# Scores of units 8 to 15 in pairs on six PSUM banks, and superblock 0's three output tiles one after another

## The chip, the cores and the metric

The kernel runs on one core of one Trainium2 chip. A core has TensorE (PE, matmuls), ScalarE (ACT), VectorE (DVE), GpSimd (POOL), and SyncE (SP), whose queue here issues nearly all DMAs. Matmuls write PSUM, which has eight banks; a bank holds 512 fp32 values in each of 128 partitions. The metric is the device time of one execution in microseconds (us). Times are medians over runs; the profile is of one execution.

## The reference

Attention with four sink keys and a window of 128, then a feed-forward layer on its output:

```python
scores = (q @ k.T) / sqrt(64)                 # 4 batches x 8 heads, 768 x 768
keep   = (key < 4) | ((0 <= row - key) & (row - key < 128))
a      = softmax(where(keep, scores, -1e9))   # over keys
x      = (a @ v), heads side by side          # 3072 x 512
h      = x @ w_in                             # 3072 x 2048
g      = h * sigmoid(beta * h)
out    = g @ w_out                            # 3072 x 512
```

## The kernel before

**Units and superblocks.** Attention is cut into 32 units: unit n is one batch, one pair of heads and one half (384 rows) of the sequence. Four units (the four head pairs) fill one superblock T = n // 4 of 384 rows of x. For each superblock there are 16 hidden groups (`hidden`: four 128x384 matmuls, L765, into one bank; `tanh` on ScalarE, L773; `gate` on VectorE, L788, which writes one slice of g) and three tiles of x @ w_out (`project`: 16 matmuls of 128x512, L815, added up in one bank, then an eviction, L823 on ScalarE or L827 on VectorE, and a store, L830). The sigmoid is taken as a tanh with beta halved, and the half is made good in the eviction.

**One unit.** Loads (L449, L457, L440), casts to bf16 on GpSimd (`cast`, L508, L511), a transpose of q and k to qkT: on TensorE for units below 12 (`transpose_in`, L531, copied out of PSUM by L540), by a DMA from unit 12 on (L515). Then the scores (64 rows, two heads side by side on the two halves of TensorE's rows), an exponential on ScalarE, a mask multiplied in on VectorE, for the second half of a sequence also the sink scores (L560, L563), `attend` (L703, L714, into the bank `av`), `normalise` (L723, L725), and a transpose of the output into xT: on TensorE (`transpose_out`, L742, copied by L746) below unit 12, by a DMA (L734) from 12 on.

**How scores are issued.** There are three forms. Units 0 to 11 use `scores` in two parts, "a" and "b": six matmuls (L587), and one exponential (L594) and one mask (L605) of 128x768 for each part. Units 12 to 15 use `scores_at_once`: eight matmuls in the four banks of `s_ps` (L624), one exponential (L631) and one mask (L680) of 128x1536. From unit 16 on `scores_pair` takes two units at a time on six banks, three for each (L660), with two exponentials (L672) and two masks (L680).

**PSUM.** Six banks are named s0, s1, tr, av, h0, h1; the other two are acc0 and acc1. Hidden groups of superblocks 0 and 1 go through acc0, acc1, h0 and h1, those of later ones through h0, h1, s0 and s1. Tiles are added up in acc0 and acc1; those of superblock 0 in acc0, acc1 and h1.

**Order.** The program is written in slots s. In one slot stand at most one hidden group, three projections, and the steps of units that fall on it (`EARLY`, `FIRST` and `STEPS`: "in", "sink", "a", "b", "av", "out"), with the casts and loads set for that slot. A planner (`Prog.order`) then lists all engines' instructions by estimated start times; what it lists is fixed when the kernel is built, and each engine runs its list in order, with semaphore waits where data or a buffer comes from another engine. In slots 0 to 31 the hidden groups of superblocks 0 and 1 run; in slots 32 to 47 superblock 0's tiles, three matmuls a slot; from 48 on hidden groups of one superblock run beside the tiles of the one before it.

Of the kernel before, what the change touches and what calls it, by code (L numbers as in the profile page):

```python
# [6 lines left out]
AF = mybir.ActivationFunctionType  # L7
# [39 lines left out]
BANK_B = {4: 's', 5: 'h', 6: 'h', 7: 'h'}  # L47
BANK_S = {4: 't', 5: 'h', 6: 'h', 7: 't'}

TURN_IN = {4: 'act', 5: 'dve', 6: 'dve', 7: 'dve', 8: 'dve', 9: 'act', 10: 'dve', 11: 'dve'}  # L50
TURN_OUT = {4: 'dve', 5: 'dve', 6: 'act', 7: 'act', 8: 'dve', 9: 'dve', 10: 'dve', 11: 'dve'}

LAST = 384

# [13 lines left out]
LATE, PAIRED = 2, 16  # L68
STEPS = {0: "in", 1: "sink", 2: "a", 3: "b", 5: "av", 7: "out"}


class Node:
# [225 lines left out]
def bass_streamingllm_window__then__act_swish_beta_kernel(  # L298
# [74 lines left out]
    def act(n):  # L373
        return {"busy": 80.0 + 0.81 * n, "lag": 140.0}
# [56 lines left out]
    def place(n):  # L431

        return n // 8, n % 4, n // 4 % 2, n % 4
# [173 lines left out]
            m[:, first:first + w].unsqueeze(1).to_broadcast([128, 2, w]), ALU.mult),  # L607
           r=[("E", n % 2, c), *names], w=[("E", n % 2, c)], **dve(780.0))

    def scores_at_once(n):  # L610

        _, _, half, pb = place(n)
        pieces = []
        for x, (kb, qb) in enumerate(BLOCKS[half]):
            if x % 4 and pieces[-1][1] == kb:
                pieces[-1] = (*pieces[-1][:3], pieces[-1][3] + 1)
            else:
                pieces.append((x, kb, qb, 1))
        with P.together("pe"):
            for x, kb, qb, nq in pieces:  # L620
                for hh in range(2):
                    rows = slice(64 * hh, 64 * hh + 64)
                    bank, at = 2 * hh + x // 4, x % 4
                    op("pe", lambda e, kb=kb, bank=bank, qb=qb, at=at, nq=nq, rows=rows: e.matmul(  # L624
                        s_ps[:, bank, 128 * at:128 * (at + nq)],
                        qkT[pb][rows, kb // 3, 1, kb % 3 * 128:kb % 3 * 128 + 128],
                        qkT[pb][rows, half, 0, qb % 3 * 128:(qb % 3 + nq) * 128], start=True, stop=True),
                       r=[("qT", pb, half), ("qkT", pb, kb // 3)], w=[("s0", "s1", "tr", "av")[bank]],
                       busy=27.0 * nq + 20.0, lag=260.0)
        z = n % 2  # L630
        op("act", lambda e: e.activation(  # L631
            E[z][:, :, :, :].rearrange("p c h x -> p c (h x)"),
            s_ps[:, :, :].rearrange("p (h b) x -> p h (b x)", h=2)[:, :, 0:768], AF.Exp,
            bias=0.0, scale=SCALE),
           x=["s0", "s1", "tr", "av"], w=[("E", z, 0), ("E", z, 1)], **act(1536))

    def scores_pair(n):

        banks = {n: ("av", "h0", "h1"), n + 1: ("s0", "s1", "tr")}
# [45 lines left out]
    def attend(n):  # L685
        _, hp, half, pb = place(n)
        z = n % 2
        where = {}
        for c, tiles in enumerate(CHUNKS[half]):
            at = 0  # L690
            for kb, qb, nq in tiles:
                for x in range(nq):
                    where[kb, qb + x] = [(c, hh, at) for hh in range(2)]
                    at += 128
        if n >= XBAR:

            where = {t: [(hh, x // 3, x % 3 * 128) for hh in range(2)]
                     for x, t in enumerate(BLOCKS[half])}
        with P.together("pe"):
            for mm in range(3):  # L700
                m, at = 3 * half + mm, mm * 2 * D1
                if half == 1:
                    op("pe", lambda e, at=at, mm=mm: e.matmul(  # L703
                        av_ps[:, at:at + 2 * D1], E_sink[z][:, mm * 128:mm * 128 + 128],
                        v_sink[:, n // 8 * 4 + hp, :, :].rearrange("p h e -> p (h e)"),
                        start=True, stop=False, skip_group_check=True),
                       r=[("E_sink", z), "v_sink", ("v_sink", 0), ("v_sink", 1)], w=["av"],
                       **pe(130))
                for hh in range(2):
                    kbs = range(m + 1) if half == 0 else (m - 1, m)  # L710
                    for x, kb in enumerate(kbs):
                        c, h2, col = where[kb, m][hh]
                        node = op("pe", lambda e, at=at, hh=hh, kb=kb, c=c, h2=h2, col=col, first=(half == 0 and x == 0),
                           last=(x == len(kbs) - 1): e.matmul(  # L714
                            av_ps[:, at + hh * D1:at + hh * D1 + D1], E[z][:, c, h2, col:col + 128],
                            v_aug[pb][:, kb, hh, :], start=first, stop=last, skip_group_check=True),
                           r=[("E", z, c), ("v_aug", pb, kb // 3)], w=["av"], **pe(65))
        return node
# [212 lines left out]
    casts = {FIRST[n - 2] + (3 if n % 2 and n - 2 >= PAIRED else 1): n for n in range(10, NU)}  # L931
    casts.update({EARLY[n - 2]["sink"]: n for n in range(6, 8)})
    slots = {*range(S_END + NM), *(at for steps in EARLY.values() for at in steps.values())}
    for s in sorted(slots):
        i = s if 0 <= s < S_P0 and s == int(s) else s - NM if S_PIPE <= s < S_END else None
# [6 lines left out]
        here += [(n, STEPS[s - FIRST[n]]) for n in range(8, NU)  # L942
                if s - FIRST[n] in STEPS and not (n >= PAIRED and n % 2 and STEPS[s - FIRST[n]] == "av")]
        here += [(n, "av") for n in range(PAIRED + 1, NU, 2) if s - FIRST[n] == 5 + LATE]
        later = []
        if i is not None and i >= S_P0 and any(n >= XBAR and step in ("sink", "b") for n, step in here):
            gate(i)
            i = None
        for n, step in here:
            half = place(n)[2]  # L950
            if step == "in" and n < XBAR:
                transpose_in(n, eng=TURN_IN.get(n, "dve"))
            if step == "sink" and half == 1:
                scores_sink(n, *((h_ps[:, 0, :], "h0") if BANK_S.get(n) == "h" else (tr_ps, "tr") if BANK_S.get(n) == "t" else (s_ps[:, 0, :], "s0") if n < PAIRED
                                 else (tr_ps, "tr")))
            if step == "b" and XBAR <= n < PAIRED:
# [6 lines left out]
            if step in ("a", "b") and n < XBAR:  # L963
# [12 lines left out]
        if s in casts:  # L976
            n = casts[s]
            cast(n)
            if n in (12, 13):
                load(n + 2)  # L980
        if s == EARLY[5]["a"]:
            for x in range(4, 8):
                cast_w(x)
# [25 lines left out]
        if s == EARLY[7]["sink"]:  # L1009
# [69 lines left out]
```

## Time and profile before

| | us |
|---|---|
| time, median of 3 runs | 225.46 (224.97 to 225.82) |
| time of the profiled execution | 225.03 |
| its span, first to last instruction | 223.2 |
| TensorE busy | 218.2 |
| ScalarE busy | 143.7 |
| VectorE busy | 128.4 |
| GpSimd busy | 74.3 |

The granted TensorE clock was 1.0 throughout. Rows of groups read: line, engine, operation, output <- inputs, shape, count; busy time and mean time of one; idle time before them and what ended it. Rows of the timeline read: start, length, engine, line, operation, output <- inputs, shape, count, and in brackets the idle time of the engine before it. The tile `six` stands for the six banks. Matmuls are pipelined, so their lengths overlap, and the distance between starts is what counts. Rows of the stages read: busy time of each engine in ten us with the number of instructions, granted clock, DMA share and GB/s. In the rows of DMA issues the last number is the median time from issue to landing.

### The profile page before, as it was taken

How to read it: one execution, taken by the hardware profiler on the slowest of the kernel's cores; microseconds unless marked ns; L12 is line 12 of the kernel's file. 1: busy time of each engine (PE TensorE's matmuls, PEld its weight loads, DVE VectorE, ACT ScalarE, POOL GpSimd, SP SyncE). 2: the span in 40 equal slices, each digit the busy share in tenths (PEclk: the TensorE clock that was granted, in tenths of full speed). 3: DMA queues.
4: the chain of work that ended last, by engine and by line, in shares of the span. 5: the costliest groups of instructions: out<-in, count | busy, mean ns of one | idle time of the engine just before them, and what ended most of it. 6: DMA issues, size and time to landing. Idle time of an engine off the chain costs nothing.

```text
span 223.2 us, 4521 instructions
## 1 busy us (share of the span) xinstructions
PE 218.2 (98%) x1757; PEld 122.1 (55%) x1757; DVE 128.4 (58%) x257; ACT 143.7 (64%) x227; POOL 74.3 (33%) x149
## 2 busy tenths in 40 slices
PE   7999999999999999999999999999999999999995
PEld 4554557555554556555565556564656555555443
DVE  5365778998734267476194448584938466254300
ACT  2777997896255477666596568596767594465411
POOL 7675767997432314453201513700000000000000
DMA  6999999997779999996996899742020202111022
GB/s 190 299 332 318 324 351 268 339 387 166 166 177 202 238 259 189 256 237 145 241 251 165 199 274 206 152 131 82 18 68 7 78 15 68 50 47 47 14 83 94
DMA packets 95437, 39.79 MB, mean 178 GB/s; under 512 B 81960, under 2 KB 88376, under 8 KB 95416
## 3 DMA queue, kind: packets, MB, share of 16 engines
q1 hardware_dynamic: 93760, 38.68, 68.6%
q10 hardware_dynamic: 1656, 0.83, 1.3%
q8 instruction: 14, 0.23, 0.4%
q14 instruction: 7, 0.06, 0.1%
HBM read 27.30 MB, written 6.29 MB: 151 GB/s over the span
## 4 chain that ended last, share of the span: by engine, by line
PE 88%; SPq 4%; DMA 3%; ACT 2%; issue 0%; DVE 0%; DVEq 0%
PE acc L815 35%; PE six L765 30%; PE acc L765 5%; PE six L714 5%; DMA wst<-in_moe_w_in_dram 3%; PE six L660 3%; SPq L457 2%; SPq L449 2%; PE six L587 2%; PE six L815 2%; PE six L703 1%; PE acc L796 1%; PE six L560 1%; PE six L531 1%; ACT th L773 1%; PE six L624 1%
## 5 line engine op out<-in xcount | busy, mean ns | idle before, releaser
L815 PE MATMUL acc<-w_out,g 128*128 128x512 bf16 x352 | 88.5, 379 | 0.0
L773 ACT ACTIVATE th<-six,beta_half 128x384 f32<-128x384 f32 x106 | 60.6, 583 | 29.8 <-PE six L765 23.9
L765 PE MATMUL six<-xT,w_in 128*128 128x384 bf16 x424 | 79.5, 326 | 0.0
L788 DVE SCALAR_TENSOR_TENSOR g<-th,six 128x384 bf16<-128x384 f32 x106 | 56.6, 550 | 26.0 <-ACT th L773 24.2
L765 PEld LDWEIGHTS six<-xT,w_in 128*128 128x128 bf16 x424 | 40.6, 98 | 29.9 <-issue 0.6
L815 PEld LDWEIGHTS acc<-w_out,g 128*128 128x128 bf16 x352 | 32.7, 98 | 33.7 <-issue 1.8
L680 DVE TENSOR_TENSOR E<-E,mask_all 128x1536 bf16<-128x1536 bf16 x20 | 19.9, 997 | 36.1 <-ACT E L672 26.8
L672 ACT ACTIVATE E<-six 128x1536 bf16<-128x1536 f32 x16 | 22.3, 1448 | 12.1 <-PE six L660 12.0
L508 POOL CAST qk<-q_stage 128x384 bf16<-128x384 f32 x32 | 16.5, 516 | 28.5 <-DMA q_stage<-in_q_dram 16.0
L511 POOL CAST v_aug<-v_stage 128x384 bf16<-128x384 f32 x32 | 17.3, 551 | 20.3 <-DMA v_stage<-in_v_dram 12.5
L594 ACT ACTIVATE E<-six 128x768 bf16<-128x768 f32 x24 | 19.1, 817 | 5.8 <-PE six L587 5.8
L508 POOL CAST qk<-k_stage 128x384 bf16<-128x384 f32 x31 | 17.3, 561 | 13.1 <-DMA k_stage<-in_k_dram 12.6
L823 ACT ACTIVATE out_sb<-acc 128x512 f32<-128x512 f32 x22 | 13.0, 595 | 10.7 <-PE acc L815 10.5
L714 PE MATMUL six<-v_aug,E 128*128 128x65 bf16 x384 | 19.3, 193 | 0.3
L714 PEld LDWEIGHTS six<-v_aug,E 128*128 128x128 bf16 x384 | 17.2, 97 | 4.0 <-ACT E L594 0.7
L765 PE MATMUL acc<-xT,w_in 128*128 128x384 bf16 x88 | 18.5, 327 | 0.3 <-DVE g L788 0.3
L725 DVE TENSOR_TENSOR o_norm<-six,rden 128x384 bf16<-128x384 f32 x32 | 17.8, 557 | 1.2
L788 DVE SCALAR_TENSOR_TENSOR g<-th,acc 128x384 bf16<-128x384 f32 x22 | 11.7, 548 | 4.6 <-ACT th L773 4.5
L773 ACT ACTIVATE th<-acc,beta_half 128x384 f32<-128x384 f32 x22 | 12.7, 591 | 2.3 <-PE acc L765 2.1
L563 ACT ACTIVATE E_sink<-six 128x384 bf16<-128x384 f32 x16 | 7.9, 497 | 5.7 <-PE six L560 5.7
L765 PEld LDWEIGHTS acc<-xT,w_in 128*128 128x128 bf16 x88 | 7.4, 97 | 4.9 <-DVE g L788 0.8
L723 DVE RECIPROCAL rden<-six 128x6 f32<-128x6 f32 x32 | 6.1, 192 | 6.6 <-PE six L714 6.5
(74 smaller groups left out, 160.0 us busy)
## 6 DMA issues: line engine op xcount, KB each, us to landing
out_dram<-out_sb SPq DMA_DIRECT2D x23, 256.0 KB, 2.6
wst<-in_moe_w_in_dram SPq DMA_DIRECT2D x8, 512.0 KB, 6.6
wst<-in_moe_w_out_dram SPq DMA_DIRECT2D x8, 512.0 KB, 8.6
q_stage<-in_q_dram SPq DMA_DIRECT2D x8, 384.0 KB, 4.0
k_stage<-in_k_dram SPq DMA_DIRECT2D x8, 384.0 KB, 4.2
v_stage<-in_v_dram SPq DMA_DIRECT2D x8, 384.0 KB, 4.4
v_stage<-in_v_dram SPq DMA_DIRECT2D x30, 96.0 KB, 4.5
q_stage<-in_q_dram SPq DMA_DIRECT2D x12, 192.0 KB, 5.0
```

Source lines behind the costliest of these rows:

```text
L508: op(eng, lambda e, x=x, name=name: e.tensor_copy(qk16[z][:, x, :, :, :], view(name)), r=[(name + "_stage", pb, half, hh) for hh in range( ...
L511: op("gp", lambda e: e.tensor_copy(v_aug[pb][:, 3 * half:3 * half + 3, :, 0:D], view("v")), r=[("v_stage", pb, half, hh) for hh in range(2 ...
L594: op("act", lambda e: e.activation(E[n % 2][:, c, :, 0:at], bank[:, 0:2, 0:at], AF.Exp, bias=0.0, scale=SCALE), x=[f"{name}0", f"{name}1"] ...
L672: op("act", lambda e, u=u, first=first: e.activation(E[u % 2][:, :, :, :].rearrange("p c h x -> p (c h x)"), six[:, first:first + 3, :].re ...
L680: op("dve", lambda e: e.tensor_tensor(both, both, mask_all[:, half, :].unsqueeze(1).to_broadcast([128, 2, 768]), ALU.mult), r=[("E", z, 0) ...
L714: last=(x == len(kbs) - 1): e.matmul(av_ps[:, at + hh * D1:at + hh * D1 + D1], E[z][:, c, h2, col:col + 128], v_aug[pb][:, kb, hh, :], sta ...
L725: op("dve", lambda e: e.tensor_tensor(o_norm[o][:, :, :, :].rearrange("p m h d -> p (m h) d"), src[:, :, 0:D], rden[z][:, :].unsqueeze(2). ...
L765: return op("pe", lambda e: e.matmul(bank, w_in16[:, c, m * 128:(m + 1) * 128], xT[:, c, T * TT:(T + 1) * TT], start=(c == 0), stop=(c == 3)),
L773: op("act", lambda e: e.activation(th[i % 3][:, :], bank, AF.Tanh, bias=0.0, scale=beta_half[:, m:m + 1]), x=[name], r=["beta"], w=[("th", ...
L788: op("dve", lambda e: e.scalar_tensor_tensor(g[T % 2][:, m, :], th[i % 3][:, :], 1.0, bank, ALU.add, ALU.mult), r=[("th", i % 3)], x=[name ...
L815: node = op("pe", lambda e: e.matmul(bank, g[T % 2][:, m, t * 128:(t + 1) * 128], w_out16[:, m, :], start=(m == 0), stop=(m == NM - 1)), r ...
L823: op("act", lambda e: e.activation(out_sb[z][:, :], bank, AF.Copy, bias=0.0, scale=0.5), x=[name], w=[("out_sb", z)], **act(NOUT))
```

## The change

- Units 8 to 15 take their scores by `scores_pair`, in pairs (8, 9), (10, 11), (12, 13) and (14, 15). `PAIRED` is 8; `scores_at_once` is gone; `attend` reads E in the pair's layout from unit 8 on.
- Superblock 0's tiles no longer run side by side on acc0, acc1 and h1, but one after another on acc1, acc0 and acc1, as those of the other superblocks do; the third is evicted by VectorE.
- The transposed q and k of units 8 to 11 are copied by ScalarE (they were VectorE's, but for unit 9's), in slots of their own (`TURNED`). The output copies of units 8 and 11 move to ScalarE.
- The slots of units from 8 on, of their casts (`CASTS`) and of some loads are set anew. The hidden groups of slots without attention steps, the weights, the transposes and the last superblock are as they were. The planner's list changes with all this.

```diff
-TURN_IN = {... 8: 'dve', 9: 'act', 10: 'dve', 11: 'dve'}
-TURN_OUT = {... 8: 'dve', 9: 'dve', 10: 'dve', 11: 'dve'}
+TURN_IN = {... 8: 'act', 9: 'act', 10: 'act', 11: 'act'}
+TURN_OUT = {... 8: 'act', 9: 'dve', 10: 'dve', 11: 'act'}
...
-FIRST = {8: 17, 9: 23, 10: 27, 11: 28}
-FIRST.update({12: 39, 13: 43, 14: 46, 15: 50, 16: 60, 17: 60})
-FIRST.update({n: (68, 76, 83, 92, 99, 108, 116)[n // 2 - 9] for n in range(18, NU)})
+TURNED = {8: 16, 9: 22, 10: 23, 11: 31}
+
+FIRST = {n: (31, 37, 42, 49, 60, 68, 76, 83, 90, 99, 106, 112)[n // 2 - 4] for n in range(8, NU)}
+CASTS = {6: EARLY[4]['sink'], 7: EARLY[5]['sink'], 10: 17, 11: 23, 12: 24, 13: 32, 14: 39, 15: 44, 16: 50, 17: 54}
+CASTS.update({n: FIRST[n - 2] + (3 if n % 2 else 1) for n in range(18, NU)})
...
-LATE, PAIRED = 2, 16
-STEPS = {0: "in", 1: "sink", 2: "a", 3: "b", 5: "av", 7: "out"}
+LATE, PAIRED = 2, 8
+STEPS = {0: "in", 1: "sink", 3: "b", 5: "av", 7: "out"}
...
-    def scores_at_once(n):
...
-        if n >= XBAR:
+        if n >= PAIRED:
             where = {t: [(hh, x // 3, x % 3 * 128) for hh in range(2)]
...
-    at = {16: 38, 17: 44, 18: 50, 19: 55, 24: 70, 25: 76, 26: 84, 27: 89}
+    at = {16: 43, 17: 44, 18: 49, 19: 55, 24: 73, 25: 78, 26: 84, 27: 85}
...
-        if i is not None and i >= S_P0 and any(n >= XBAR and step in ("sink", "b") for n, step in here):
+        if i is not None and i >= S_P0 and any(n >= PAIRED and step in ("sink", "b") for n, step in here):
             gate(i)
...
-            if step == "b" and XBAR <= n < PAIRED:
-                scores_at_once(n)
-                later.append(lambda n=n: mask_at_once(n))
             if step == "b" and n >= PAIRED and n % 2 == 0:
                 scores_pair(n)
...
-        if s == 34:
+        if s == 33:
...
-        if S_P0 <= s < S_PIPE:
-
-            for t, (bank, name, eng) in enumerate(
-                    ((acc[0][:, :], "acc0", "act"), (acc[1][:, :], "acc1", "act"),
-                     (h_ps[:, 1, :], "h1", "dve"))):
-                done = project(0, t, s - S_P0, bank, name, eng)
-        elif s >= S_PIPE:
-            T = (s - S_PIPE) // NM + 1
+        if s >= S_P0:
+            T = (s - S_P0) // NM
             for x in range(3 * (s % NM), 3 * (s % NM) + 3):
                 a = (3 * T + x // NM + 1) % 2
...
-                done = project(T, x // NM, x % NM, acc[a][:, :], f"acc{a}")
+                done = project(T, x // NM, x % NM, acc[a][:, :], f"acc{a}",
+                               "dve" if T == 0 and x // NM == 2 else "act")
```

More of the change, by code (lines that the diff above doesn't have):

```diff
@@ L48 @@
 BANK_S = {4: 't', 5: 'h', 6: 'h', 7: 't'}
-TURN_IN = {4: 'act', 5: 'dve', 6: 'dve', 7: 'dve', 8: 'dve', 9: 'act', 10: 'dve', 11: 'dve'}
-TURN_OUT = {4: 'dve', 5: 'dve', 6: 'act', 7: 'act', 8: 'dve', 9: 'dve', 10: 'dve', 11: 'dve'}
+TURN_IN = {4: 'act', 5: 'dve', 6: 'dve', 7: 'dve', 8: 'act', 9: 'act', 10: 'act', 11: 'act'}
+TURN_OUT = {4: 'dve', 5: 'dve', 6: 'act', 7: 'act', 8: 'act', 9: 'dve', 10: 'dve', 11: 'act'}
 LAST = 384
@@ L608, in mask @@
            r=[("E", n % 2, c), *names], w=[("E", n % 2, c)], **dve(780.0))
-    def scores_at_once(n):
[L612 to L635, printed above, removed]
     def scores_pair(n):
@@ L926, in bass_streamingllm_window__then__act_swish_beta_kernel @@
         sink_keys(n, ended)
-    at = {16: 38, 17: 44, 18: 50, 19: 55, 24: 70, 25: 76, 26: 84, 27: 89}
+    at = {16: 43, 17: 44, 18: 49, 19: 55, 24: 73, 25: 78, 26: 84, 27: 85}
     loads = {t + 2 * x: (n, name) for n, t in at.items() for x, name in enumerate("qkv")}
-    casts = {FIRST[n - 2] + (3 if n % 2 and n - 2 >= PAIRED else 1): n for n in range(10, NU)}
-    casts.update({EARLY[n - 2]["sink"]: n for n in range(6, 8)})
     slots = {*range(S_END + NM), *(at for steps in EARLY.values() for at in steps.values())}
@@ L941, in bass_streamingllm_window__then__act_swish_beta_kernel @@
         here = [(n, step) for n in EARLY for step in EARLY[n] if EARLY[n][step] == s]
-        here += [(n, STEPS[s - FIRST[n]]) for n in range(8, NU)
-                if s - FIRST[n] in STEPS and not (n >= PAIRED and n % 2 and STEPS[s - FIRST[n]] == "av")]
-        here += [(n, "av") for n in range(PAIRED + 1, NU, 2) if s - FIRST[n] == 5 + LATE]
+        here += [(n, "in") for n in TURNED if TURNED[n] == s]
+        for n in range(8, NU):
+            step = STEPS.get(s - FIRST[n] - (LATE if n % 2 and s - FIRST[n] >= 5 else 0))
+            if step in ("sink", "b", "av") or step == "out" and n < XBAR:
+                here.append((n, step))
         later = []
-        if i is not None and i >= S_P0 and any(n >= XBAR and step in ("sink", "b") for n, step in here):
+        if i is not None and i >= S_P0 and any(n >= PAIRED and step in ("sink", "b") for n, step in here):
             gate(i)
@@ L962, in bass_streamingllm_window__then__act_swish_beta_kernel @@
                 later.append(lambda n=n: mask_at_once(n + 1))
-            if step in ("a", "b") and n < XBAR:
+            if step in ("a", "b") and n < PAIRED:
                 scores(n, "ab".index(step), *((h_ps, "h") if BANK_B.get(n) == "h" and step == "b" else (s_ps, "s")))
@@ L975, in bass_streamingllm_window__then__act_swish_beta_kernel @@
                     transpose_out(n, eng=TURN_OUT.get(n, "dve"))
[L976 to L980, printed above, removed]
+        for n in CASTS:
+            if CASTS[n] == s:
+                cast(n)
+                if n in (12, 13):
+                    load(n + 2)
         if s == EARLY[5]["a"]:
```

## The prediction

> **What bounds the kernel now.** I read the page first: busy times, the 40 slices, the chain that ended last and the two largest groups.
>
> ```profile
> span 223.2 us, 4521 instructions
> PE 218.2 (98%) x1757; PEld 122.1 (55%) x1757; DVE 128.4 (58%) x257; ACT 143.7 (64%) x227; POOL 74.3 (33%) x149
> PE   7999999999999999999999999999999999999995
> PE 88%; SPq 4%; DMA 3%; ACT 2%; issue 0%; DVE 0%; DVEq 0%
> L815 PE MATMUL acc<-w_out,g 128*128 128x512 bf16 x352 | 88.5, 379 | 0.0
> L765 PE MATMUL six<-xT,w_in 128*128 128x384 bf16 x424 | 79.5, 326 | 0.0
> ```
>
> TensorE (PE) has work in every slice after the first, is 88% of the chain, and its two big matmul groups show no idle time before them. A busy share says little about pipelined matmuls, so next came the timeline of TensorE alone, by start times: from one row's start to the next is what the first one cost.
>
> ```profile
> 39.53 0.81 PE L765 MATMUL six<-xT,w_in 128*128 128x384 bf16 x4
> 40.27 0.34 PE L587 MATMUL six<-qkT 64*128 64x384 bf16 x2
> 40.54 0.34 PE L531 MATMUL six<-ident,qk 128*128 128x128 bf16 x3
> 40.72 1.46 PE L765 MATMUL acc<-xT,w_in 128*128 128x384 bf16 x8
> ...
> 56.35 0.81 PE L815 MATMUL six<-w_out,g 128*128 128x512 bf16 x3
> 57.09 0.34 PE L587 MATMUL six<-qkT 64*128 64x256 bf16 x4
> 57.36 0.54 PE L714 MATMUL six<-v_aug,E 128*128 128x65 bf16 x12
> ...
> 62.48 0.38 PE L815 MATMUL six<-w_out,g 128*128 128x512 bf16 x1
> 62.79 0.50 PE L624 MATMUL six<-qkT 64*128 64x128 bf16 x8
> 63.23 0.60 PE L815 MATMUL acc<-w_out,g 128*128 128x512 bf16 x2
> ...
> 90.83 1.67 PE L815 MATMUL acc<-w_out,g 128*128 128x512 bf16 x7
> 92.44 0.83 PE L660 MATMUL six<-qkT 64*128 64x256 bf16 x14
> 93.21 2.98 PE L815 MATMUL acc<-w_out,g 128*128 128x512 bf16 x13
> 96.02 0.53 PE L714 MATMUL six<-v_aug,E 128*128 128x65 bf16 x12
> 96.39 1.24 PE L815 MATMUL acc<-w_out,g 128*128 128x512 bf16 x5
> 97.47 2.76 PE L765 MATMUL six<-xT,w_in 128*128 128x384 bf16 x16
> 100.06 0.53 PE L714 MATMUL six<-v_aug,E 128*128 128x65 bf16 x12
> ...
> 116.62 1.67 PE L815 MATMUL acc<-w_out,g 128*128 128x512 bf16 x7
> 118.23 0.84 PE L660 MATMUL six<-qkT 64*128 64x256 bf16 x18
> 119.00 2.98 PE L815 MATMUL acc<-w_out,g 128*128 128x512 bf16 x13
> ```
>
> No row brackets an idle time: here TensorE waits for nobody. A 128x512 matmul costs 2.81/13 = 0.216 us (93.21 to 96.02), a 128x384 one 2.59/16 = 0.162 (97.47 to 100.06), three transposes 0.18 (40.54 to 40.72), a whole `attend` 0.37 (96.02 to 96.39). So this stage is worth what its TensorE instructions cost, and a change gains only by issuing cheaper ones, and only while nobody makes TensorE wait.
>
> **What the change does to TensorE.** Up to the row at 39.53 both kernels issue the same instructions, on every compute engine and on SP's queue. After it, the counts of hidden matmuls, projections, transposes and `attend` are unchanged; what changes is how scores are issued. A score matmul has 64 rows, and each stretch of them costs more than its columns, where TensorE enters and where it leaves it:
>
> - `scores`, first part: the four matmuls at 39.53 cost 4 x 0.162, to 40.18; the transposes start at 40.54: 0.36. Second part: 57.36 - (56.35 + 3 x 0.216) = 0.36. Units 8 to 11 have two each: 8 x 0.36 = 2.88 us.
> - `scores_at_once`: 63.23 - (62.48 + 0.216) = 0.534. Units 12 to 15: 4 x 0.534 = 2.14 us.
> - `scores_pair`, both forms: 93.21 - (90.83 + 7 x 0.216) = 0.865 with 14 matmuls, 119.00 - (116.62 + 7 x 0.216) = 0.865 with 18. It replaces two units at a time, four times: 3.46 us.
>
> Sum: 2.88 + 2.14 - 3.46 = **1.56 us less**. It is all fixed cost: a first part's 384 columns, two row groups side by side, would need 0.162 us, so some 0.2 us per stretch is entering and leaving, and 12 stretches become 4 (8 x 0.2 = 1.6).
>
> The Trainium skill says why there is such a cost: in "TensorEngine Tiling (Array Packing)", section Tiling Modes, changing the tiling mode drains TensorE. "TensorE: Matmul & The Clock Gate", section Single matmul latency, puts the fixed part of a lone warm matmul at about 166 ns; as an estimate from these pages, 16 switches fewer would be worth 2.7 us and give 222.8 before any stall. The rows, 0.2 for a switch in and out together, decide for 1.56.
>
> **What must stay covered.** After a pair, ScalarE and VectorE of the kernel before go:
>
> ```profile
> 93.26 2.79 ACT L672 ACTIVATE E<-six 128x1536 bf16<-128x1536 f32 x2 [1.64 <-PE six L660]
> 94.74 0.96 DVE L680 TENSOR_TENSOR E<-E,mask_all 128x1536 bf16<-128x1536 bf16 x1 [2.54 <-ACT E L672]
> 96.08 1.16 DVE L680 TENSOR_TENSOR E<-E,mask_all 128x1536 bf16<-128x1536 bf16 x1 [0.38 <-ACT E L672]
> 97.45 0.56 DVE L725 TENSOR_TENSOR o_norm<-six,rden 128x384 bf16<-128x384 f32 x1
> 66.03 0.69 DVE L827 TENSOR_SCALAR out_sb<-six 128x512 f32<-128x512 f32 x1
> ```
>
> Counted from the pair's end (93.21): exponentials done at +1.48 and +2.84, first mask at +2.49, second at +4.03, normalisation at +4.80. The order in which the changed kernel issues shows what covers them:
>
> - 8/9: thirteen projections (2.81) before `attend(8)`, against +2.49. Eight more and `attend` bring the transposes of unit 8's output to +4.91, against +4.80. Free, by 0.1 to 0.3.
> - 10/11: now the 0.69 us eviction of tile 2 stands between the two masks on VectorE, and the mask, reciprocal and normalisation queue behind it. First mask to +2.49, eviction to +3.2, second mask to +4.3, normalisation to about +5.2; `attend(11)`, which rewrites that bank, is reached at 21 x 0.216 + 0.37 + 0.16 = +5.07. A stall of about 0.15.
> - 12/13: `attend(12)` at +2.81, `attend(13)` after +5.6, the first hidden group at +4.4: free. 14/15: eight projections (1.73), then a hidden group in a bank that the first exponential leaves at +1.48: free by 0.25.
> - Four pairs together: 0.15, between nothing and one late normalisation (0.56) in each, 2.2; I take 0.15, since three margins are above zero.
>
> Before the first pair, eight part exponentials and their masks are gone, while the copies of all four transposed inputs go to ScalarE:
>
> ```profile
> 40.00:50.00 10.00, 10.00 (x86) 5.66 (x84) 9.37 (x21) 9.46 (x18) 9.44 (x14) 1.00 1.01 365
> 45.49 0.80 ACT L540 COPY qkT<-six 128x768 bf16<-128x768 bf16 x1
> 46.17 0.60 ACT L773 ACTIVATE th<-acc,beta_half 128x384 f32<-128x384 f32 x1
> 46.65 0.60 ACT L773 ACTIVATE th<-six,beta_half 128x384 f32<-128x384 f32 x1
> 51.60 1.08 POOL L496 CAST w_out<-wst 128x1024 bf16<-128x1024 f32 x1 [0.22 <-DMA wst<-in_moe_w_out_dram]
> ```
>
> A copy costs 46.17 - 45.49 = 0.68 us of ScalarE, a tanh 0.48. From 40.18 TensorE needs 13 x 4 x 0.162 = 8.4 for hidden groups and three sets of six transposes (2 x 0.18 each), together 9.5 us; ScalarE needs 13 x 0.48 + 4 x 0.68 = 9.0. Tight, but four banks hold the backlog: 0 to 0.5 us, I take 0.05.
>
> **Weights and queues.** Tile 0 now runs through all sixteen pieces of w_out at once. Nine projections follow the transposes, so the first pair starts at about 40.18 + 9.5 + 9 x 0.216 = 51.6 and ends at 52.5; piece 14 of tile 0 is reached 8 x 0.216 later, at 54.2. The last w_out cast ends at 52.68 (the 51.60 row): 1.5 us to spare, and GpSimd has only lost a small key copy ahead of it. If that cover went, every us would count whole. On SP's queue two output stores move ahead of the transposes for units 14 and 15, and the output transposes of 12 and 13 ahead of those for 16 and 17:
>
> ```profile
> 70.24 1.93 SPq L515 DMA_TRANSPOSE qkT<-qk  x1
> 81.74 2.44 SPq L515 DMA_TRANSPOSE qkT<-qk  x1
> 78.01 1.05 SPq L830 DMA_DIRECT2D out_dram<-out_sb  x2
> qkT<-qk SPq DMA_TRANSPOSE x20, 3.9
> ```
>
> Unit 15's transpose (70.24, lands 3.9 later) with two stores of 0.53 lands at 75.2, and the pair 14/15 stands at 80.5 in the sum of TensorE's order. Unit 17's (81.74) waits for the normalisation of 13, some 2 us: 88, for a pair at 96.5. The later pairs come 1 to 5 us earlier than before. All hidden, at 5 us or more.
>
> **The sum.** 225.03 - 1.56 + 0.15 + 0.05 = 223.67 for the profiled execution, which stands 0.43 under the median of the runs (225.46). Against the median: 225.46 - 1.36 = **224.1 us** (-0.6%).
>
> **The rivals.**
>
> - *Evacuation eats the gain.* Until +1.48 after a pair all six score banks are taken, until +2.84 three of them, and little but projections can run. If every pair lost about 0.3 us to a late mask or normalisation (0.56 rows, margins of 0.1 to 0.25), and the copy stretch 0.4, then 1.6 would go: 225.5, no change. For it: the 10/11 sum above is over already. Against: the same chain after the pairs at 92.44 and 118.23 ends in time. The Trainium skill names this ("TensorEngine Tiling (Array Packing)", Performance Considerations, PSUM Bottleneck): tiling does not speed up evacuation, which may become the bottleneck; the rows after 93.21 show it covered.
> - *Late weights: slower.* If w_out's last cast ends later than 54.2, TensorE stands at tile 0's piece 14, while before three tiles shared each piece and the late ones were wanted later. It decides from a cast 1.5 + 1.36 = 2.9 us late (55.5); one that ends at 56.8 gives 225.46 - 1.36 + (56.8 - 54.2) = 226.7. For it: the last cast waited for its DMA (0.22). Against: everything ahead of it is as before.
> - *The gain is bigger.* If TensorE's switches cost more where they are alone than among projections, up to 1 us more: 223.1. The rows of three forms agree at 0.2, so little speaks for it.
> - *Nothing changes.* If the pairs were hidden work, 225.5. Against: TensorE has no idle to hide them in.
>
> **How the numbers follow.** Forecast 0.64 (own range 223.5 to 224.6), evacuation 0.22 (224.6 to 225.8), late weights or another late transfer 0.08 (225.8 to 228), bigger gain 0.05, nothing 0.01. Range for 8 in 10: 223.3, the full 1.56 with the runs' spread below the median (0.5, to 224.97), to 225.6, by which most of the second case ends. About 0.5% (1.13 us) can be told from no change. The forecast lies close to that bound (224.33): 0.07 of its 0.64 and nearly all of the second case fall inside. Faster 0.62, same 0.28, slower 0.10.
>
> **What would show it.** Right: four L660 stretches between 51 and 82, each 0.865 from the projection's end to the next; no L587 after 40; the first pair at 51.6, the second at 60.2, 16/17 at 96.5 where the order now puts it; TensorE's end 1.36 earlier. Wrong: idle before `attend(11)` or the transposes of o_norm above 0.3; `L815 <- POOL w_out` among TensorE's waits; a pair that waits for a qkT DMA; ScalarE still copying when the first pair is due.

## The result, and the profile after

The changed kernel takes **223.51 us** in the median of 20 runs (222.92 to 226.78) against 224.89 for the kernel before on the same chip (224.36 to 227.08, 20 runs): a ratio of **0.9945, 95% interval 0.9919 to 0.9972**. A second set of runs gave 0.9919 (0.9900 to 0.9939). Both ratios compare the means of the runs without slow executions, of which this kernel has 7 in 32 runs and the kernel before none in 38; with all runs the two ratios would be 0.996 and 1.000. The profiled execution took 223.19 us, its span 221.5 us: 1.84 and 1.7 us less than before.

The page of the changed kernel; its line numbers are 25 lower than before in most of the code (L790 was L815, L740 was L765, L635 was L660):

```profile
span 221.5 us, 4552 instructions
PE 216.5 (98%) x1765; PEld 123.1 (56%) x1765; DVE 124.5 (56%) x248; ACT 145.9 (66%) x228; POOL 74.2 (34%) x149
PE   7999999999999999999999999999999999999995
PE 94%; ACT 4%; DVE 0%; issue 0%; DVEq 0%
L790 PE MATMUL acc<-w_out,g 128*128 128x512 bf16 x368 | 88.7, 379 | 0.0
L740 PE MATMUL six<-xT,w_in 128*128 128x384 bf16 x424 | 79.5, 326 | 0.0
```

TensorE is the bound as before, now 94% of the chain. Its share has stayed at 98%: both its work and the span have become shorter. The timeline of TensorE alone (start, duration, line, operation, count):

```profile
51.62 0.83 PE L635 MATMUL six<-qkT 64*128 64x256 bf16 x14
52.39 2.98 PE L790 MATMUL acc<-w_out,g 128*128 128x512 bf16 x13
55.20 0.53 PE L689 MATMUL six<-v_aug,E 128*128 128x65 bf16 x12
...
57.29 0.33 PE L717 MATMUL six<-ident,o_norm 128*128 128x128 bf16 x3
...
60.24 0.83 PE L635 MATMUL six<-qkT 64*128 64x256 bf16 x14
61.01 2.98 PE L790 MATMUL acc<-w_out,g 128*128 128x512 bf16 x13
...
66.08 0.53 PE L689 MATMUL six<-v_aug,E 128*128 128x65 bf16 x12
...
69.67 0.84 PE L635 MATMUL six<-qkT 64*128 64x256 bf16 x18
...
80.54 0.84 PE L635 MATMUL six<-qkT 64*128 64x256 bf16 x18
...
96.54 0.83 PE L635 MATMUL six<-qkT 64*128 64x256 bf16 x14
```

No row brackets an idle time. Four pairs stand between 51 and 82 us, the first at 51.62, the second at 60.24, and 16/17 at 96.54, where the prediction has 51.6, 60.2 and 96.5. Summed from the end of the matmul ahead of each stretch to the start of the one behind, the 64-row stretches behind 40 us cost 11.96 us before (20 of them) and 10.37 after (12): **1.59 us less**, out of 1.73 between a row that both kernels share (the stretch at 33.39 us) and the last matmul. The other 0.14 is in steps of some hundredths; I have not put it down to rows. What stood beside the pairs, from the timelines of the other engines, with the one row of the view by stretches of time (PE, PEld, DVE, ACT, POOL busy, then the granted clock):

```profile
49.99 0.79 ACT L542 COPY qkT<-six 128x768 bf16<-128x768 bf16 x1
50.73 1.04 POOL L498 CAST w_out<-wst 128x1024 bf16<-128x1024 f32 x1 [0.23 <-DMA wst<-in_moe_w_out_dram]
53.92 0.96 DVE L655 TENSOR_TENSOR E<-E,mask_all 128x1536 bf16<-128x1536 bf16 x1 [3.24 <-ACT E L647]
56.36 0.56 DVE L700 TENSOR_TENSOR o_norm<-six,rden 128x384 bf16<-128x384 f32 x1
62.54 0.96 DVE L655 TENSOR_TENSOR E<-E,mask_all 128x1536 bf16<-128x1536 bf16 x1 [2.70 <-ACT E L647]
63.42 0.68 DVE L802 TENSOR_SCALAR out_sb<-acc 128x512 f32<-128x512 f32 x1
64.02 0.95 DVE L655 TENSOR_TENSOR E<-E,mask_all 128x1536 bf16<-128x1536 bf16 x1
65.10 0.56 DVE L700 TENSOR_TENSOR o_norm<-six,rden 128x384 bf16<-128x384 f32 x1
40.00:50.00 10.00, 10.00 (x74) 6.35 (x73) 7.78 (x15) 9.55 (x19) 9.08 (x14) 1.00 1.06 368
```

The margins: mask of unit 8 done at 54.88, `attend(8)` at 55.20 (0.32); normalised at 56.92, transposes at 57.29 (0.37); unit 10 normalised at 65.66, `attend(11)` at 66.08 (0.42). The last copy ends at 50.78, the first pair starts at 51.62. The last w_out cast ends at 51.77; tile 0 reaches that piece at 54.12.

### The profile page after: what moved, and what is told of

Same layout as the page of the kernel before. It is cut to its first block, busy times and chain, and to the rows that moved or that the text cites. A ratio compares the mean times of both kernels' runs of the same rounds, so it can differ in the third digit from the quotient of the medians.

```text
span 221.5 us, 4552 instructions
## 1 busy us (share of the span) xinstructions
PE 216.5 (98%) x1765; PEld 123.1 (56%) x1765; DVE 124.5 (56%) x248; ACT 145.9 (66%) x228; POOL 74.2 (34%) x149
## 4 chain that ended last, share of the span: by engine, by line
PE 94%; ACT 4%; DVE 0%; issue 0%; DVEq 0%
PE acc L790 36%; PE six L740 31%; PE acc L740 6%; PE six L689 5%; PE six L635 4%; ACT E L596 3%; PE six L581 2%; PE acc L850 2%; PE six L589 1%; PE six L678 1%; PE six L533 1%; PE acc L771 1%; PE six L562 1%; ACT th L748 1%; PE six L717 1%; PE acc L533 0%
## 5 line engine op out<-in xcount | busy, mean ns | idle before, releaser
L790 PE MATMUL acc<-w_out,g 128*128 128x512 bf16 x368 | 88.7, 379 | 0.0
L740 PE MATMUL six<-xT,w_in 128*128 128x384 bf16 x424 | 79.5, 326 | 0.0
L740 PEld LDWEIGHTS six<-xT,w_in 128*128 128x128 bf16 x424 | 40.2, 98 | 28.1 <-issue 0.2
L790 PEld LDWEIGHTS acc<-w_out,g 128*128 128x128 bf16 x368 | 34.6, 98 | 36.9 <-issue 1.3
L655 DVE TENSOR_TENSOR E<-E,mask_all 128x1536 bf16<-128x1536 bf16 x24 | 23.8, 991 | 39.9 <-ACT E L647 39.9
L647 ACT ACTIVATE E<-six 128x1536 bf16<-128x1536 f32 x24 | 33.5, 1448 | 14.2 <-PE six L635 14.2
L510 POOL CAST qk<-q_stage 128x384 bf16<-128x384 f32 x32 | 18.1, 568 | 31.4 <-DMA q_stage<-in_q_dram 21.8
L513 POOL CAST v_aug<-v_stage 128x384 bf16<-128x384 f32 x32 | 16.7, 538 | 14.6 <-DMA v_stage<-in_v_dram 7.7
L510 POOL CAST qk<-k_stage 128x384 bf16<-128x384 f32 x31 | 16.7, 539 | 14.3 <-DMA k_stage<-in_k_dram 12.3
L740 PE MATMUL acc<-xT,w_in 128*128 128x384 bf16 x88 | 18.6, 327 | 0.3 <-DVE g L763 0.3
L596 ACT ACTIVATE E<-six 128x768 bf16<-128x768 f32 x16 | 12.6, 818 | 2.7 <-PE six L589 2.7
L740 PEld LDWEIGHTS acc<-xT,w_in 128*128 128x128 bf16 x88 | 7.7, 98 | 5.2 <-DVE g L763 0.8
L635 PEld LDWEIGHTS six<-qkT 64*128 64x128 bf16 x192 | 7.2, 94 | 5.2 <-issue 3.4
L635 PE MATMUL six<-qkT 64*128 64x128 bf16 (+2 forms) x192 | 10.0, 244 | 0.0
```

The costliest lines, as they stand in the source:

```text
L510: op(eng, lambda e, x=x, name=name: e.tensor_copy(qk16[z][:, x, :, :, :], view(name)), r=[(name + "_stage", pb, half, hh) for hh in range( ...
L513: op("gp", lambda e: e.tensor_copy(v_aug[pb][:, 3 * half:3 * half + 3, :, 0:D], view("v")), r=[("v_stage", pb, half, hh) for hh in range(2 ...
L596: op("act", lambda e: e.activation(E[n % 2][:, c, :, 0:at], bank[:, 0:2, 0:at], AF.Exp, bias=0.0, scale=SCALE), x=[f"{name}0", f"{name}1"] ...
L635: pb=pb, half=half: e.matmul(six[:, bank, 128 * at:128 * (at + nq)], qkT[pb][rows, kb // 3, 1, kb % 3 * 128:kb % 3 * 128 + 128], qkT[pb][r ...
L647: op("act", lambda e, u=u, first=first: e.activation(E[u % 2][:, :, :, :].rearrange("p c h x -> p (c h x)"), six[:, first:first + 3, :].re ...
L655: op("dve", lambda e: e.tensor_tensor(both, both, mask_all[:, half, :].unsqueeze(1).to_broadcast([128, 2, 768]), ALU.mult), r=[("E", z, 0) ...
```

## The experiments

All twelve runs in one table. "Trace" is the time from the shared row at 33.4 us to the last matmul, less the same time in the changed kernel (185.33 us; before 187.06, so +1.73): it leaves out what executions differ by at their start. e11 lacks that row and is measured from another one (its section).

| run | ratio to before (95%) | trace, us |
|---|---|---|
| e1 changed kernel again | 0.9919 (0.9900 to 0.9939) | +5.08, with one stop of 3.3 us |
| e2 pairs in two | 1.0064 (1.0038 to 1.0090) | +3.59 |
| e3 pairs in three | 1.0243 (1.0219 to 1.0267) | +6.57 |
| e4 tiles only | 1.0056 (1.0035 to 1.0076) | +2.47 |
| e5 pairs only for 12 to 15 | 0.9992 (0.9961 to 1.0023) | +1.75 |
| e6 pairs only for 8 to 11, with the tiles | 0.9950 (0.9921 to 0.9979) | +0.94 |
| e7 masks twice | 1.0181 (1.0121 to 1.0241) | +6.83 |
| e8 w_out casts twice | 1.0198 (1.0132 to 1.0264) | +6.39 |
| e9 two matmuls twice, inside | 0.9999 (0.9979 to 1.0018) | +2.09 |
| e10 the same, apart | 1.0093 (1.0072 to 1.0114) | +3.81 |
| e11 parts of 5 to 7 together | 1.0008 (0.9988 to 1.0028) | +1.43, from an earlier row |
| e12 copies on VectorE | 1.0025 (0.9991 to 1.0060) | +0.75 |

**What a stretch costs.** The theory: TensorE pays for entering and leaving each stretch of 64-row matmuls. The rival: the gain is relief of VectorE and ScalarE, or the order of the tiles. First more stretches, at the same work.

```diff
 placed = self.order()                     # emit: for each pair, the projection
+placed.pop(last)                          # just ahead of it (in three: two)
+pair.guests.insert(0, guest)
...
-for k, (fn, dma, before) in enumerate(n.items):
+items.insert(len(n.items) * (x + 1) // (len(n.guests) + 1), (guest.id, 0, guest.items[0]))
+for owner, k, (fn, dma, before) in items:
```

> The changed kernel with the last projection ahead of each of the twelve score pairs moved into the middle of that pair, so that each stretch of 64-row matmuls becomes two. All five engines issue the same instructions, and the four others in the same order. Theory (a stretch costs some 0.2 us for entering and leaving): 12 more stretches, +2.4 us against the changed kernel (2.0 to 2.8), 1.0 us over the kernel before; each pair's cost rises from 0.865 to about 1.06 us beside the projection. Rival (the gain came from relief of VectorE and ScalarE, or from the order of the tiles; a stretch costs nothing by itself): within 0.3 us of the changed kernel.

> As the one before, with two projections inside each pair, at a third and at two thirds. Theory: 24 more stretches, +4.8 us against the changed kernel (4.0 to 5.6), twice the step of one projection. Rival: within 0.3 us. If the cost were not of entering and leaving but of the two row groups standing unequal at the cut, the two steps would differ by more than 0.5 us.

The timeline of TensorE in the kernel with pairs in two:

```profile
95.72 2.97 PE L805 MATMUL acc<-w_out,g 128*128 128x512 bf16 x13
98.62 0.55 PE L649 MATMUL six<-qkT 64*128 64x256 bf16 x7
99.11 0.39 PE L805 MATMUL acc<-w_out,g 128*128 128x512 bf16 x1
99.43 0.55 PE L649 MATMUL six<-qkT 64*128 64x128 bf16 x7
99.92 1.25 PE L805 MATMUL acc<-w_out,g 128*128 128x512 bf16 x5
```

A cut pair costs 99.92 - (95.72 + 13 x 0.216) - 0.216 = 1.18 us against 0.865: 0.31 more with 14 matmuls, 0.26 with 18. Over twelve pairs +3.40 us, in three parts +6.56. The steps are nearly equal, so it is a price per stretch, and no engine but TensorE had its order changed: the rival's 0.3 us falls. But 0.28 is more than the 0.2 forecast, and both sums lie above the ranges that I had given (2.0 to 2.8 and 4.0 to 5.6). A cut also leaves the two row groups unequal, so the next two runs kept that apart: the first two score matmuls of a pair are issued twice, in e9 both times inside the pair, in e10 the first time ahead of it as a stretch of their own.

```diff
+one = (n.guests[0].id, 0, n.guests[0].items[0])      # the projection ahead of the pair
+twice = [(n.id, k, item) for k, item in enumerate(n.items[:2])]
+items = [one] + twice + items             # e9, inside
+items = twice + [one] + items             # e10, apart
```

> The changed kernel with the first two score matmuls of each of the twelve pairs issued twice in a row, inside the pair (the second writes what the first wrote). No stretch is added: only the columns count, 128 to 256 per row group, side by side. All theories expect +0.05 to 0.15 us per pair, 0.6 to 1.8 us in all. It is the base for the next kernel.

> The same two matmuls issued twice, but the first time one projection ahead of the pair, so that they are a stretch of their own. The difference from the kernel before this one is the price of entering and leaving a stretch alone. Theory of the prediction: 0.2 us each (0.15 to 0.25), 2.4 us for twelve. If the 0.28 us measured when pairs were cut held no imbalance of the row groups: 3.4 us. Rival (a stretch costs nothing): 0.

TensorE's timeline at one pair, inside and then apart:

```profile
95.70 2.54 PE L806 MATMUL acc<-w_out,g 128*128 128x512 bf16 x11
98.17 0.94 PE L650 MATMUL six<-qkT 64*128 64x256 bf16 x16
99.04 1.90 PE L806 MATMUL acc<-w_out,g 128*128 128x512 bf16 x8
```

```profile
95.69 2.11 PE L806 MATMUL acc<-w_out,g 128*128 128x512 bf16 x9
97.73 0.28 PE L650 MATMUL six<-qkT 64*128 64x256 bf16 x2
97.94 0.39 PE L806 MATMUL acc<-w_out,g 128*128 128x512 bf16 x1
98.26 0.83 PE L650 MATMUL six<-qkT 64*128 64x256 bf16 x14
99.03 1.90 PE L806 MATMUL acc<-w_out,g 128*128 128x512 bf16 x8
```

Inside: 99.04 - (95.70 + 11 x 0.216) = 0.964, 0.10 over a plain pair: columns alone. Apart: 99.03 - (95.69 + 9 x 0.216) - 0.216 = 1.18. The difference, **0.22 us, is the price of entering and leaving one stretch**, the same in all twelve pairs. Over twelve pairs e10's rows give 3.84, which accounts for its +3.81. (e9's +2.09 holds 1.24 for its pairs and, by starts, a stop of 0.62 us ahead of 35.6 us, for a gate and ahead of the first edited pair; 0.2 is left.) The runs agree, though e10 has only two: 1.0093 less 0.9999 is 2.1 us, or 0.18 a pair. The 0.04 to 0.09 us by which a cut in the middle of a pair costs more than this was not taken apart. With 384 columns at 0.162 us, the short stretches of the kernel before hold 0.20 (a part) and 0.21 (`scores_at_once`) beside their columns, a pair 0.22: 8 x 0.20 + 4 x 0.21 - 4 x 0.22 = 1.56.

**The parts of the change, one at a time.**

```diff
-        if S_P0 <= s < S_PIPE:            # the kernel before
...
-            for t, (bank, name, eng) in enumerate(((acc[0]...), (acc[1]...), (h_ps[:, 1, :], "h1", "dve"))):
-                done = project(0, t, s - S_P0, bank, name, eng)
+        if s >= S_P0:                     # the changed kernel's loop
+            T = (s - S_P0) // NM
...
```

> The kernel before with one part of the change: superblock 0's three tiles of x @ w_out follow each other on two accumulators; scores as before. Theory: the same TensorE instructions in another order, so the same time as the kernel before, within 0.3 us either way. Rival (the order of the tiles, or the bank that it sets free, brings the gain): 0.8 us or more under it. Rival (late weights, which the pairs only hide): over 0.5 us above it, with TensorE waiting for GpSimd's casts of w_out.

The stretches cost what they did. Two waits of TensorE for another engine are new; here with the mask that the first waits for (PE and DVE of the timeline):

```profile
121.16 2.12 PE L815 MATMUL acc<-w_out,g 128*128 128x512 bf16 x9
122.69 0.96 DVE L680 TENSOR_TENSOR E<-E,mask_all 128x1536 bf16<-128x1536 bf16 x1 [2.65 <-ACT E L672]
123.71 0.29 PE L714 MATMUL six<-v_aug,E 128*128 128x65 bf16 x4 [0.38 <-DVE E L680]
124.77 0.59 PE L815 MATMUL acc<-w_out,g 128*128 128x512 bf16 x2 [0.25 <-ACT out_sb L823]
```

Behind this pair stand nine projections instead of thirteen, because a tile of x @ w_out ends there; nine take 1.9 us, and the mask is there 2.5 us after the pair. So `attend` waits 0.38 for the mask, and the next tile 0.25 for an eviction that queues behind two exponentials on ScalarE (by starts 0.54 and 0.20). The tiles' new order by itself is no gain: 0.74 us slower than before by the trace, where I had expected at most 0.3, and slower by the runs. It is not late weights: no row of TensorE waits for w_out.

```diff
-FIRST.update({12: 39, 13: 43, 14: 46, 15: 50, 16: 60, 17: 60})        # the kernel before
+FIRST.update({12: 45, 13: 45, 14: 50, 15: 50, 16: 60, 17: 60})
...
-LATE, PAIRED = 2, 16
+LATE, PAIRED = 2, 12
...
+    casts.update({39: 14, 43: 15, 50: 16, 54: 17})
```

> The kernel before, with units 12 to 15 in two score pairs instead of four scores_at_once, placed behind tile 2's last projection so that h1 is free; units 8 to 11 and the order of the tiles as before. Theory (stretches priced singly): 4 x 0.534 - 2 x 0.865 = 0.41 us less TensorE work; TensorE's end 0.41 us earlier plus whatever waits it shows. Rival (the gain belongs to units 8 to 11 and to ScalarE and VectorE's relief there): 0 from the stretches.

The two new pairs cost 0.87 each, as priced, 0.40 us less than four `scores_at_once`. And the kernel is no faster (+0.02 us against before), because behind the later pair 16/17 a tile now ends with the thirteenth projection, just ahead of `attend(16)`, while the accumulator that the next tile needs is evicted behind the pair's two exponentials (PE, the weight loads of PE, and ACT):

```profile
97.83 1.09 ACT L823 ACTIVATE out_sb<-acc 128x512 f32<-128x512 f32 x2
98.72 1.24 PE L815 MATMUL acc<-w_out,g 128*128 128x512 bf16 x5 [0.27 <-ACT out_sb L823]
100.04 0.42 PEld L714 LDWEIGHTS six<-v_aug,E 128*128 128x128 bf16 x12 [0.58 <-DVE o_norm L725]
```

A wait for the eviction and one for a normalisation: by TensorE's starts they cost 0.22 and 0.25 there, which is the rival of evacuation, and it ate this part's gain of 0.40 whole.

```diff
+FIRST.update({12: 45, 13: 48, 14: 51, 15: 54})                        # the changed kernel
...
+            if step == "b" and 12 <= n < 16:
+                scores_at_once(n)
+                later.append(lambda n=n: mask_at_once(n))
```

> The changed kernel with units 12 to 15 back on scores_at_once, each in a slot of its own; units 8 to 11 stay in pairs. Theory: 8 x 0.36 - 2 x 0.865 = 1.15 us less in the stretches than the kernel before, 0.41 more than the changed kernel, plus whatever waits it shows. Rival (the tiles' new order brings the gain): no slower than the changed kernel.

The stretches give 1.18 us less than before (1.15 expected); waits of under 0.4 us each, the largest of an `attend` for its mask, take back 0.4. Its 0.79 us under before and 0.94 over the changed kernel agree with stretches that add up, 1.18 and 0.40, and with covers that do not. The runs alone don't tell it from the changed kernel (0.9950 against 0.9945 and 0.9919).

```diff
-TURN_IN = {..., 8: 'act', 9: 'act', 10: 'act', 11: 'act'}             # the changed kernel
+TURN_IN = {..., 8: 'dve', 9: 'act', 10: 'dve', 11: 'dve'}
```

> The changed kernel with the copies of the transposed inputs of units 8, 10 and 11 back on VectorE, where the kernel before had them. VectorE has 7.78 us of work between 40 and 50 us in the changed kernel, and three copies of 0.9 us bring it to 10.5: more than the time there is. If the backlog in the banks covers that, within 0.2 us of the changed kernel, and the move of the copies had no part in the result; if not, TensorE waits for gates or for qkT, 0.3 to 1.0 us in all.

From the timeline of DVE and PE:

```profile
46.23 0.95 DVE L542 COPY qkT<-six 128x768 bf16<-128x768 bf16 x1
47.70 1.15 PE L740 MATMUL acc<-xT,w_in 128*128 128x384 bf16 x6 [0.32 <-DVE g L763]
```

A copy of 0.95 us stands ahead of a gate on VectorE, and TensorE waits for the gate; by starts it loses 0.48 us there, 0.64 between 34 and 50 us and 0.75 in all. So the move of the copies to ScalarE is a part that the gain needs: without it nearly half would have gone by the trace. The four runs lie far apart (224.00, the one of the trace, 224.12, 226.24 and 226.30 us), and by their interval all of it could have gone.

**The cover behind the pairs.**

```diff
         op("dve", lambda e: e.tensor_tensor(both, both, mask, ALU.mult), ...)   # mask_at_once
+        if n < 16:
+            op("dve", lambda e: e.tensor_tensor(both, both, mask, ALU.mult), ...)
```

> The changed kernel with each mask of units 8 to 15 applied twice (0.95 us more of VectorE per unit; a mask of ones and zeros, so the values stay). The four other engines issue the same in the same order. It measures the cover behind the pairs. With the margins read from the changed kernel's rows (attend of the first unit 0.3 us, the transposes or the second attend 0.4 us): first attend some 0.6 us late in each of four pairs, the second or the transposes 0.4 to 0.9 us: 3.5 to 4.5 us in all over the changed kernel. If the cover were as thin as the rival of evacuation had it (margins gone): 6 us or more. If the cover were wide: under 1 us.

```profile
55.06 0.96 DVE L660 TENSOR_TENSOR E<-E,mask_all 128x1536 bf16<-128x1536 bf16 x1
56.08 0.54 PE L694 MATMUL six<-v_aug,E 128*128 128x65 bf16 x12 [0.71 <-DVE E L660]
59.27 0.34 PE L722 MATMUL six<-ident,o_norm 128*128 128x128 bf16 x3 [0.93 <-DVE o_norm L705]
70.17 0.54 PE L694 MATMUL six<-v_aug,E 128*128 128x65 bf16 x12 [1.03 <-DVE o_norm L705]
```

The sum, 6.83 us, was above what I expected, and by itself it would speak for the case in which the margins are gone (6 us or more). The rows decide otherwise: the masks end later than by the 0.95 us that I had reckoned with, since the first of unit 8 takes 1.11 us instead of 0.96 and the two of unit 9 take 1.26 and 1.28 (last section), and the margins themselves hold. The mask of unit 8 is 56.02 - 54.88 = 1.14 late; `attend(8)` starts 0.88 late, so 0.26 was spare (read from the rows: 0.32). The normalisation ahead of `attend(11)` ends at 70.12 against 65.66, 4.46 later, and `attend(11)` starts 4.09 later: 0.37 spare (read: 0.42). The changed kernel is covered by three or four tenths of a microsecond and no more.

```diff
         op("gp", lambda e: e.tensor_copy(dst, view), ...)                       # cast_w
+        if i >= 10:
+            op("gp", lambda e: e.tensor_copy(dst, view), ...)
```

> The changed kernel with six of the eight casts of w_out done twice on GpSimd, in the same order: the last then ends near 56.3 us instead of 51.8. Theory: tile 0 reaches the last piece at 54.1, so TensorE waits for GpSimd by about 2.2 us (1.7 to 2.7) and ends that much later. Rival (the planner or other work hides late weights): under 0.5 us.

From the timelines of PE and POOL, and the view by stretches of time (the granted clock is the number behind the five engines):

```profile
53.87 1.81 POOL L501 CAST w_out<-wst 128x1024 bf16<-128x1024 f32 x1
55.74 0.61 PE L793 MATMUL acc<-w_out,g 128*128 128x512 bf16 x2 [1.98 <-POOL w_out L501]
58.55 1.76 PE L793 MATMUL acc<-w_out,g 128*128 128x512 bf16 x5 [2.21 <-POOL w_out L501]
60.00:62.00 2.00, 1.83 (x15) 1.11 (x15) 0.75 (x2) 0.00 (x0) 1.53 (x5) 0.50 0.45 102
```

The rival of late weights is real: with the cover gone TensorE waits for GpSimd, twice, 4.2 us by the brackets and 4.5 by starts. I had expected 2.2, from casts of 0.98 us; two of them took 1.81 and 1.76. On top of the waits came a slow stretch at half the clock. Whether the kernel before would have borne the same late weights was not tried: there late casts would also have delayed unit 12's inputs.

**One step further.** If a stretch costs 0.2 us, units 5 to 7 have three to spare.

```diff
-         7: {... 'b': 12.5, ...}}              # EARLY
+         7: {... 'b': 10.5, ...}}
...
+            if step == "b" and n in (5, 6, 7):
+                scores_both(n)            # part 0 into s_ps, part 1 into h_ps, one group
-            if step in ("a", "b") and n < PAIRED:
+            elif step in ("a", "b") and n < PAIRED and n not in (5, 6, 7):
```

> The changed kernel with the two score parts of units 5, 6 and 7 issued as one stretch each (into the banks that the parts had), so three stretches fewer between 20 and 35 us. Theory: 3 x 0.2 = 0.6 us under the changed kernel (-0.25%), if TensorE still waits for nobody there; the exponentials of both parts now follow each other, so up to 0.6 us could come back as a wait of attend for them, and then it is no faster.

From e11's timelines of DVE and PE:

```profile
27.05 0.95 DVE L542 COPY qkT<-six 128x768 bf16<-128x768 bf16 x1
28.52 0.82 PE L774 MATMUL acc<-xT,w_in 128*128 128x384 bf16 x4 [0.33 <-DVE g L797]
```

And from the view by stretches of time of the changed kernel (PE, PEld, DVE, ACT, POOL busy):

```profile
20.00:30.00 10.00, 9.51 (x100) 5.22 (x101) 6.79 (x13) 9.92 (x20) 6.58 (x11) 1.00 1.09 366
```

No faster than before, and so slower than the changed kernel. The stretches cost what they should: 0.53 us for a stretch that holds both parts of a unit, against twice 0.37. But from a stretch that both kernels have (at 21.24 us here, at 20.15 in the changed kernel) to the last matmul e11 takes 200.00 us against 198.57. Between 26 and 45 us TensorE's starts show eight delays of 0.12 to 0.50 us that the changed kernel does not have, 1.9 us together, against 0.6 saved. The largest is the row above: it waits for a gate that stands behind a copy on VectorE, as in e12. Here TensorE is not alone the bound (ScalarE is busy 9.92 us of the ten in the changed kernel), and a stretch that is saved returns as waits. No version beat the changed kernel.

**The changed kernel again.**

> The changed kernel once more, beside the three kernels that are compared with it. The theory (eight fewer stretches of 64-row matmuls on TensorE, some 0.2 us each) and every rival expect what was measured: about 0.55% under the kernel before, a profiled span of 221.5 us, and no wait on TensorE after 40 us.

The ratio agrees. The profiled execution does not: its span is 227.0 us, and TensorE's timeline shows a wait behind 40 us:

```profile
149.52 1.78 PE L740 MATMUL six<-xT,w_in 128*128 128x384 bf16 x5 [3.29 <-DMA xT<-o_norm]
```

It waited 3.29 us for a transposed output, which took 5.02 us to land (144.45 to 149.47); in the other execution the same transpose took 2.31 and landed 2.1 us before its weight load. The prediction had worked out margins for the transposes of the inputs only. The place is as narrow in the kernel before (1.9 us to spare), and why the transpose took longer in this execution stays open.

## Why the prediction was right

The forecast was 0.6% under before, and the ratio is 0.9945. The predicted 224.1 us lies 0.6 us above the measured 223.51 mostly because it was set against the 225.46 us of three runs, while twenty runs gave 224.89.

- *TensorE is the bound, and waits for nobody behind 40 us*: right in the changed kernel's first execution; in e1's it waited once, for a transpose. e11 shows where it ends: ahead of 35 us the same saving is worth nothing.
- *1.56 us less in the stretches, 0.2 us for each*: right. Measured 1.59 in the rows, 0.22 for a stretch alone (e10 less e9), and e5 and e6 show the two halves adding up (0.40 and 1.18). The Trainium skill ("TensorEngine Tiling (Array Packing)", Tiling Modes) has it that a change of mode drains TensorE; these runs agree that a switch has a price. The estimate that took 166 ns for each of sixteen switches (2.7 us, 222.8) was too high: 0.22 us is the price of both switches of a stretch.
- *8/9, 12/13 and 14/15 free*: right, no row of TensorE waits behind these pairs; 0.32 and 0.37 us were spare at 8/9, and e7 finds 0.26 of the 0.32 by taking it away.
- *10/11 stalls by 0.15*: the step that failed. I let the second mask follow the eviction to "+4.3" and the normalisation to "about +5.2". The rows give +3.96 and +4.65 (64.97 and 65.66 less 61.01), while `attend(11)` came at +5.07 as forecast. Of the 0.55 us, 0.11 is the eviction, which ends at +3.09; 0.23 is the mask, which took 0.95 us and not the 1.16 of the row that I had taken as typical; and 0.21 is the reciprocal and normalisation, for which I allowed 0.9 and which ended 0.69 behind the mask. The row of 1.16 stands beside a cast on GpSimd (95.92 to 96.43), and so was no price of a mask alone (last section). In the changed kernel too a GpSimd instruction stands beside that mask, but there it was the one that took longer (64.06, 0.96 us against 0.20 elsewhere). Had the mask taken 1.16, the normalisation would have ended near +4.9, still ahead of +5.07.
- *The copies on ScalarE cost 0.05*: nothing is seen of it. What I had not asked is what they are there for. On VectorE they would have cost 0.75 us by e12's trace, half the forecast gain; I had priced the move as a risk only, not as a condition.
- *Late weights, 1.5 us to spare*: 2.35 were (51.77 to 54.12). "Every us would count whole" was too kind: behind 4.5 us of waiting came 1.7 more (e8).
- *Evacuation eats the gain*: not here, by 0.3 to 0.4 us. But e4 and e5 are that rival, with its rows. Each did one part alone, and the planner let a tile end just ahead of an `attend`, nine or thirteen projections behind its pair. A chance of 0.22 for it was not too much.
- *The bigger gain, and nothing changes*: both fall with the price of 0.22 us.

The sum by its terms: 225.03 - 1.59 gives 223.44 for the profiled execution; it took 223.19. Of the 0.48 by which the forecast 223.67 was high, 0.20 is the two stalls that did not come, 0.03 the stretches, 0.14 the small steps in TensorE's order, and the rest lies outside the time from the shared row to the last matmul.

## What to carry to other kernels

Where TensorE has no idle time, count its changes of row count, not only its columns: a stretch of 64-row matmuls among 128-row ones cost 0.22 us beside its columns, whatever its length, and issuing two units in one stretch halves that. Before gathering, add up what must happen behind the longer stretch (exponential, mask, normalisation, eviction) against the matmuls that stand behind it in the order: 2.81 us of them covered a mask at 2.49, 1.9 us did not. And where a part of a change looks idle, ask what the engine it relieves would have done: three copies were, by the trace, nearly half the gain.

## What was not expected of the hardware

- *A stop costs more than its length.* After e8's waits (1.98 and 2.21 us with two matmuls between them) the granted clock was 0.50 from 60 to 62 us, with TensorE at work again. TensorE's starts slip by 4.5 us at the two waits and by 1.7 more in the following 10 us. e1's wait of 3.29 us cost 4.8 in all, with a granted clock of 0.50 from 149 to 152 us. The Trainium skill, "TensorE: Matmul & The Clock Gate", Part 1, says that the clock goes to half after an idle window of about 3.4 us; the traces agree in kind, though none of e8's waits is that long by itself. That a wait of 0.71 us in e7 costs 0.88 by starts is something else, a matter of reading: the bracket counts from the end of the row before, and a 128x512 row lasts 0.38 us where the next can start 0.216 behind it.
- *VectorE's mask and GpSimd's cast hold each other up.* In e8 a w_out cast took 1.81 us beside masks (1.04 alone), and one of these masks 1.32 (0.96 alone). The Trainium skill, "SBUF — State Buffer", Who interferes with whom, says that a VectorE instruction with two SBUF inputs contends with a GpSimd instruction that reads SBUF, which is what both are; the trace agrees. It is part of why the casts ended later than I had worked out. In all the traces a 128x1536 mask with no GpSimd instruction beside it takes 0.96 us, and each one over 1.0 stands beside one. In DVE's timeline of e8:

```profile
55.17 1.32 DVE L658 TENSOR_TENSOR E<-E,mask_all 128x1536 bf16<-128x1536 bf16 x1 [0.38 <-ACT E L650]
```

- *Executions differ before the change begins.* The shared row stands at 33.39 us in the two kernels' first profiles and between 33.10 and 34.52 in the others that have it. Differences under 1 us were therefore read from that row on, not from spans.
